# The products for h as three float32r products of split operands in place of a 20-product scheme in float32

## The chip, the core and the metric

The kernel runs on one core of one Trainium2 chip. The metric is the device time of one execution in microseconds (us). TensorE (PE) multiplies matrices out of SBUF into PSUM, which has eight banks of 128 x 512 float32; VectorE (DVE) and ScalarE (ACT) do elementwise work, GpSimd (POOL) and SyncE (SP) mostly issue DMAs. Each engine works through its own queue in order, and the queues meet only at semaphores.

## The reference

A causal convolution of seven taps over 8 sequences of 4096 tokens with 192 channels, with softmax-normalized weights for each of 8 heads of 24 channels; then a two-layer network on the 32768 tokens:

```
w = exp(weight - max); w = w / (sum(w) + 1e-9)              # 8 heads x 7 taps
y[b, s, head, :] = sum_k w[head, k] * x_pad[b, s + k, head, :]
h = y @ w_in                                                # 192 -> 2048
g = h * 1 / (1 + exp(-h))                                   # SiLU
out = g @ w_out                                             # 2048 -> 192
```

The weights w_in and w_out are handed in as 64-bit floats, x and the taps as 32-bit floats; the output is float32.

## The kernel before

The 32768 tokens are worked off in 32 stages of 1024 tokens (two halves of 512). Channels lie on partitions: x is loaded by DMA into `nat` (`load`), turned by VectorE into `xt` (`turn_in`, L617), and convolved (`conv`, L645): one product on ScalarE and six multiply-adds on VectorE for each of three slices of 64 channels, both token halves on the 128 partitions together.

*h.* The 192 input channels are three slices of 64, and the products use half the rows of the array each: two such products run beside each other on rows 0 to 63 and 64 to 127. For each of four groups g of 512 hidden columns the plain way has 24 products of 64 x 128 by 64 x 512; the kernel has 20 (`PRODUCT`, L146, issued by `product`, L725), in the manner of fast matrix multiplication. For that it forms sums of slices of x (`spread` and `win`, into `dup` and `win`), holds sums of slices of the weights (`w_own`, `w_other`, made once by `combine`), and adds and copies the products in PSUM (`micro`, L740, with the table `MICRO`), before SiLU on ScalarE writes g. Everything is native float32.

*out.* g is kept in `g_all` as 8 slots for each of two pairs of groups, of 1024 columns. Another 20-product scheme: 13 sums of slots for each pair (`SUMS`, `sum_g`, L782), 20 products for each pair (`OUT`, `out_slot`, L794), each four matrix products of 128 x 64 by 128 x 256 on column halves of the array, and 24 zeroings, copies and additions (`Dz`, `Dk`, `Dh`, `Di` ...) around them, then six turns on VectorE and eight stores. Seven of the 26 sums are not made by VectorE but by DMAs that add, issued by GpSimd (`BY_DMA`, L298).

*Order.* The instructions of a stage are written out as tokens in `PLAN` (L63): a product P, a sum s, an out product Q, a convolution tap v and so on, with a sign for the stage that it belongs to (`-` the one before, `+` the next). `step` (L862) issues them one after another, and `pin` holds each engine to that order, so the stages overlap only as the list says. The first stage is plain (`up_plain`, `down_plain`: all 24 products), since the weights are still being rounded from 64-bit words by integer operations on VectorE (`rounded`, L461) and combined; `START` (L87) is a list of its own for the passage from there into the plan. PSUM banks are handed round (`at`, L319): a bank goes back after its last use.

## Time and profile before

| | |
|---|---|
| median of three runs | 2310.18 us (2310.01 to 2311.09) |
| profiled execution, first to last instruction | 2307.9 us |
| what the median has beyond that span | 2.3 us |
| PE busy | 2288.8 us, 99% |
| VectorE busy | 2128.4 us, 92% |
| ScalarE busy | 1503.1 us, 65% |
| GpSimd busy | 234.8 us, 10% |
| granted TensorE clock | 0.997 |

All durations come from one profiled execution. A record of TensorE lasts from the first column that enters to the last result that leaves, so records overlap, and their pace is read from start to start. A float32 matrix product of the program is two records, each with its own weight load (PEld). "L730" is a line of the kernel before; the pair "64*128" names the rows and columns of the array that a product uses.

### The profile page before, as it was taken

What the parts mean: (1) busy time and instruction counts of PE and PEld (TensorE: products, weight loads), DVE (VectorE), ACT (ScalarE), POOL (GpSimd) and SP (SyncE); (2) the same over time, 40 slices, a digit from 0 to 9 for tenths busy, and PEclk for the clock granted to TensorE, in tenths of its full rate; (3) what the DMA queues carried; (4) which work ended last, traced back from release to release, by engine and by line L of the source; (5) the groups of instructions that cost most, each with busy time, mean ns of one, the idle gap of its engine ahead of it and who ended that gap; (6) DMA issues with size and microseconds to landing.
All of it is one profiled execution on the core that took longest, in us unless ns stands there. A gap on an engine that the chain in (4) does not pass through costs nothing.

```text
span 2307.9 us, 40513 instructions
## 1 busy us (share of the span) xinstructions
PE 2288.8 (99%) x15334; PEld 1377.7 (60%) x15334; DVE 2128.4 (92%) x3140; ACT 1503.1 (65%) x2957; POOL 234.8 (10%) x301
## 2 busy tenths in 40 slices
PE   9899999999999999999999999999999999999998
PEld 5255656655656656566556566566665565665664
DVE  8999999999999999999999999999999999999976
ACT  5277666676666776666776667766667766677653
POOL 4300011000011000111000110001110001100001
PEclk9999999999999999999999999999999999999999
DMA  7133355433555433555334554335553345543345
GB/s 174 26 71 74 64 104 104 85 70 68 89 104 103 76 68 66 102 104 94 68 69 81 103 103 76 72 70 93 104 98 70 69 75 103 104 80 69 71 78 92
DMA packets 465525, 195.73 MB, mean 85 GB/s; under 512 B 422000, under 2 KB 427120, under 8 KB 465328
## 3 DMA queue, kind: packets, MB, share of 16 engines
q0 software_dynamic: 31696, 115.36, 27.0%
q1 hardware_dynamic: 429440, 77.25, 19.2%
q8 instruction: 120, 1.97, 0.3%
q10 hardware_dynamic: 4192, 0.52, 0.2%
q14 instruction: 77, 0.63, 0.1%
HBM read 31.46 MB, written 25.17 MB: 25 GB/s over the span
## 4 chain that ended last, share of the span: by engine, by line
PE 95%; DVE 3%; DMA 1%; issue 0%; SPq 0%; ACT 0%; DVEq 0%; ACTq 0%; POOLq 0%
PE ps L730 48%; PE ps L800 46%; DVE u L309 2%; DVE nat L654 1%; DMA nat<-in_x_dram 1%; DMA g<-g 0%; PE ps L818 0%; DVE wd L309 0%; SPq L349 0%; DVE xt L620 0%; DMA dup<-nat 0%; DVE win L683 0%; DVE dup L683 0%; SPq L452 0%; DVE fin L775 0%
## 5 line engine op out<-in xcount | busy, mean ns | idle before, releaser
L800 PE MATMUL ps<-g,wd 128*64 128x256 f32 x9920 | 1091.3, 380 | 0.2
L800 PEld LDWEIGHTS ps<-g,wd 128*64 128x64 f32 x9920 | 703.8, 137 | 415.6 <-issue 25.8
L792 DVE TENSOR_TENSOR g<-g 128x1024 f32<-128x1024 f32 x589 | 702.0, 1218 | 24.1 <-PE ps L800 8.0
L730 PE MATMUL ps<-win,w_own 64*128 64x512 f32 x1488 | 658.4, 599 | 7.1 <-DVE win L683 6.4
L730 PE MATMUL ps<-dup,w_other 64*128 64x512 f32 x1240 | 513.0, 598 | 0.0
L730 PE MATMUL ps<-dup,w_own 64*128 64x512 f32 x1240 | 487.4, 595 | 0.0
L730 PE MATMUL ps<-win,w_other 64*128 64x512 f32 x992 | 475.1, 596 | 0.3 <-ACT g L764 0.3
L654 DVE SCALAR_TENSOR_TENSOR nat<-xt,turned,nat 128x512 f32<-128x512 f32 x558 | 399.7, 745 | 0.9 <-ACT nat L651 0.9
L766 ACT ACTIVATE ps<-ps 128x512 f32<-128x512 f32 (+1 forms) x465 | 254.3, 547 | 208.0 <-PE ps L800 175.6
L777 ACT ACTIVATE g<-ps 128x512 f32<-128x512 f32 x620 | 364.1, 603 | 18.0 <-DVE g L780 10.8
L780 DVE TENSOR_TENSOR g<-g,ps 128x512 f32<-128x512 f32 x496 | 331.1, 680 | 11.6 <-PE ps L730 8.2
L730 PEld LDWEIGHTS ps<-win,w_own 64*128 64x128 f32 x1488 | 251.4, 186 | 148.4 <-issue 61.5
L730 PEld LDWEIGHTS ps<-dup,w_own 64*128 64x128 f32 x1240 | 203.4, 186 | 140.7 <-issue 46.5
L780 DVE TENSOR_TENSOR ps<-u,ps 128x512 f32<-128x512 f32 x372 | 254.0, 691 | 33.4 <-PE ps L730 16.5
L786 POOL DMA_DIRECT2D g<-g x217 | 187.7, 913 | 945.8 <-DVE g L792 369.4
L764 ACT COPY u<-ps 128x512 f32<-128x512 f32 x341 | 200.1, 588 | 52.6 <-PE ps L730 48.7
L730 PEld LDWEIGHTS ps<-dup,w_other 64*128 64x128 f32 x1240 | 189.8, 185 | 71.4 <-ACT ps L766 42.4
L730 PEld LDWEIGHTS ps<-win,w_other 64*128 64x128 f32 x992 | 179.8, 186 | 85.3 <-issue 65.3
L777 ACT ACTIVATE g<-g 128x512 f32<-128x512 f32 x372 | 211.4, 625 | 4.5 <-DVE g L780 3.0
L766 ACT ACTIVATE fin<-ps 128x256 f32<-128x256 f32 x93 | 35.5, 382 | 214.7 <-PE ps L800 214.7
L780 DVE TENSOR_TENSOR fin<-fin,ps 128x256 f32<-128x256 f32 x248 | 94.1, 409 | 85.9 <-PE ps L800 84.7
L764 ACT COPY ps<-ps 128x512 f32<-128x512 f32 (+1 forms) x217 | 120.5, 556 | 73.8 <-PE ps L800 57.6
(92 smaller groups left out, 1166.8 us busy)
## 6 DMA issues: line engine op xcount, KB each, us to landing
g<-g POOLq DMA_DIRECT2D x217, 512.0 KB, 5.2
nat<-in_x_dram SPq DMA_DIRECT2D x382, 64.0 KB, 3.3
out_dram<-fin SPq DMA_DIRECT2D x244, 96.0 KB, 5.0
dup<-nat SPq DMA_DIRECT2D x97, 128.0 KB, 2.3
win<-nat SPq DMA_DIRECT2D x62, 128.0 KB, 2.3
fin<-in_moe_w_in_dram SPq DMA_DIRECT2D x8, 192.0 KB, 5.0
w_other<-w_own POOLq DMA_DIRECT2D x8, 192.0 KB, 7.3
g<-in_moe_w_out_dram SPq DMA_DIRECT2D x4, 384.0 KB, 7.0
```

The source lines that it names most:

```text
L309: return lambda *args, **kw: pin(getattr(self.engine, name)(*args, **kw))
L654: nc.vector.scalar_tensor_tensor(out=dst, in0=src, scalar=tap, in1=dst, op0=ALU.mult, op1=ALU.add)
L730: nc.tensor.matmul(at(b, "bank", to, g), raw(g, w, e), rows(slot_of(b, x_), e), start=first, stop=True, skip_group_check=True,)
L764: pin(nc.scalar.copy(seen[to], seen[u]))
L766: pin(nc.scalar.activation(seen[to], seen[u], AF.Copy, scale=-1.0))
L777: pin(nc.scalar.activation(seen[to], seen[u], AF.Silu, scale=float(sign)))
L780: pin(nc.vector.tensor_tensor(seen[to], seen[u], seen[v], op=op))
L786: nc.gpsimd.dma_start(out=flat(g_all[:, q, to]), in_=flat(g_all[:, q, u + v - to]), accum_op=ALU.add)
L792: pin(nc.vector.tensor_tensor(to, u, v, op=ALU.add if sign > 0 else ALU.subtract))
L800: nc.tensor.matmul(acc[R * h : R * h + R, 0:HT], wd[:, 2 * q + e, w, :], g_all[:, q, slot, e, ts(h, HT)], start=False, stop=True, skip_gro ...
```

## The change

The h products no longer use the 20-product scheme. Each value of y and of w_in is split into a high part of 12 bits and the rest, and kept three times, in the type float32r: the high part (index 0), the low part (1; for the weights times 4096) and a scaled difference (2). For each tile of h the product of the parts 0 and the product of the parts 1 are added in a PSUM bank (token A for the first 128 channels, C for the last 64), ScalarE multiplies the bank by 1 + 1/4096 in place (X), the product of the parts 2 is added (B for 128 channels, E for 64), and ScalarE applies SiLU (S). Written out, that is the whole product. A and B use the whole array; C and E use 64 rows for each token half, beside each other. A tile of h is 128 columns by 512 tokens; there are 32 in a stage (group j, chunk c, half n), so a stage has 32 tokens each of A, B, X and S, and 16 each of C and E.

The first 128 channels of x are now one tile over all 1024 tokens (`nat0`, `xt0`, `xs0`), the last 64 one with the two token halves on the partition halves (`nat1` ...). The convolution has six multiply-adds of 1024 columns and six of 512. `split` makes the three parts of y: one product on ScalarE (hx), a subtraction (lx) and a multiply-subtract (dx) on VectorE. The sums of x, the sums of weights of w_in and all additions and copies for h are gone. `round_in` splits the weights of a group after rounding them, and for the last 64 channels copies them to the other rows by DMA.

The out products, their sums, and their additions are as before, but all 26 sums of g are on VectorE. The token order of the stage is new. `START` is gone: the first stage is three-product for h and plain for out, then the whole convolution of the second stage comes, and the plan runs from stage 1 on.

```diff
     PLAN = (
+        "A.000 A.010 +i.1 -Dj9.0 A.021 A.011 A.020 A.001 C.02 +ha.2 C.01 +v.10 -s11.1 X.021 C.00  "
+        "dx.0 X.010 +ld.1 X.020 X.011 -Q4.1 +ld.0 X.001 +ld.3 -Q17.0 -Q4.0 -Q17.1 X.000 E.01  "
+        "E.02 E.00 -Di14_9.0 B.011 B.021 -DS15.0 B.020 -Di12_9.0 -Di17_f.0 A.031 S.021 B.001  "
+        "A.101 A.030 B.000 S.011 +i.0 B.010 A.100 S.001 S.020 A.120 +v.00 S.000 A.121 C.12 C.03  "
+        "S.010 +v.11 C.10 +v.01 A.110 +v.02 X.120 A.111 X.121 X.100 X.101 +v.03 X.031 X.030  "
+        "B.121 B.120 B.100 B.101 E.12 +v.12 S.120 E.10 C.11 S.100 X.111 S.121 X.110 E.03 B.031  "
+        "A.201 S.031 B.030 S.101 A.210 +v.04 B.111 A.211 E.11 C.21 S.030 X.210 A.131 A.130 A.200  "
+        "B.110 C.13 C.20 S.111 X.211 S.110 -DS16.0 E.21 B.210 A.220 -DS13.0 B.211 A.221 X.131  "
+        "C.22 -DS14.0 -DS12.0 X.200 X.201 X.130 S.210 E.13 E.20 X.220 B.131 s1.0 B.201 B.130  "
+        "S.211 A.311 X.221 S.131 B.220 A.230 S.201 B.221 A.231 C.23 E.22 +v.05 S.130 X.231 S.220  "
+        "A.301 A.310 X.230 B.231 B.200 A.300 S.221 +v.13 C.30 S.200 X.300 E.23 +v.14 C.31 S.231  "
+        "B.230 S.230 A.331 X.301 A.320 A.330 -st.0 X.311 +v.06 X.310 A.321 +v.15 C.33 C.32 E.30  "
+        "E.31 B.310 X.330 X.331 s0.0 s2.0 X.320 X.321 B.300 B.301 B.311 B.330 B.331 B.320  "
+        "-DS17.0 S.310 +v.16 Dz0.0 S.311 B.321 E.33 E.32 S.321 S.300 s1.1 Dz3.0 Dz1.0 S.331  "
+        "S.330 Q0.0 Q11.0 Q13.0 S.320 s4.0 Q13.1 s2.1 s0.1 Q0.1 Dk15.0 S.301 Q16.0 s3.0 Q16.1  "
+        "Q2.1 Q19.0 s4.1 +hx.0 s6.0 Dk11.0 Q2.0 s3.1 Q18.1 Q19.1 Q11.1 Q1.1 s6.1 s8.0 Q18.0 s7.0  "
+        "Q14.0 Q1.0 Q8.1 +hx.1 Q8.0 s8.1 *ha.0 s9.1 Q14.1 Dk8.0 Q7.1 Q9.0 Q3.0 s7.1 +lx.1 Q9.1  "
+        "Q7.0 Dh12.0 s9.0 *ld.6 Q3.1 s10.0 *ld.7 Dk5.0 s10.1 s5.0 Q12.0 Q12.1 Di12_7.0 s5.1  "
+        "Dh15.0 Q15.1 Q6.0 +dx.1 Q6.1 -st.1 s12.0 Dh13.0 s11.0 Dk13.0 s12.1 Di15_f.0 *ld.5 Q15.0  "
+        "Dh17.0 *ld.4 Q5.1 Dh16.0 +lx.0 Dh14.0 *ha.1 *ld.2 Q10.1 Q10.0 Q5.0 Di16_11.0 Du9.0  "
+        "Di14_f.0 Di13_f.0"
     )
...
-    BY_DMA = ('s0.1', 's11.1', 's4.0', 's4.1', 's5.0', 's5.1', 's8.1')
+    BY_DMA = ()
...
+    nats = [const.tile([P, n, SQ], F32, name=f"nat{i}") for i, n in enumerate((TT // SQ, TB // SQ))]
+    xts = [const.tile([P, pad + n], F32, name=f"xt{i}") for i, n in enumerate((TT, TB))]
+    xs = [const.tile([P, 3, n], F32R, name=f"xs{i}") for i, n in enumerate((TT, TB))]
+    w_a = const.tile([P, 3, NJ, 4, P], F32R, name="w_a")
+    w_b = const.tile([P, 3, NJ, 4, P], F32R, name="w_b")
...
+    def load(b, i, queue):
+        i, small = i % 4, i // 4
+        dst = nats[small][SQ * i : SQ * i + SQ]
+        if small:
+            c = P + SQ * (i % 2)
+            queue.dma_start(out=dst, in_=x_v[2 * b + i // 2][:, :, c : c + SQ])
+        else:
+            queue.dma_start(out=dst, in_=x_w[b][:, :, SQ * i : SQ * i + SQ])
...
+    def round_in(j, part, shared, scaled_by_act):
+        lo, hi = (0, CA) if part == 0 else (CA, WC)
+        words = raw(("i", j))[:, 2 * lo : 2 * hi].rearrange("p (x c t) -> p x c t", x=2, t=2)
+        w = scratch[:, 3 * WC : 3 * WC + hi - lo]
+        rounded(w.rearrange("p (x c) -> p x c", x=2), words, shared, scaled_by_act)
+        low = rest[:, 0 : hi - lo]
+        if part == 0:
+            parts = [(slice(0, P), slice(0, 4))]
+        else:
+            parts = [(slice(R * a, R * a + R), slice(2 * a, 2 * a + 2)) for a in range(2)]
+        for p_, c_ in parts:
+            to = [flat(ws[part][p_, v, j, c_, :]) for v in range(3)]
+            act.activation(to[0], w[p_], AF.Copy, scale=BELOW)
+            vec.tensor_tensor(low[p_], w[p_], f32(to[0]), op=ALU.subtract)
+            act.activation(to[1], low[p_], AF.Copy, scale=SPLIT)
+            vec.scalar_tensor_tensor(
+                out=to[2], in0=f32(to[0]), scalar=1.0 / SPLIT, in1=low[p_], op0=ALU.mult, op1=ALU.subtract
+            )
+        if part:
+            for a in range(2):
+                pool.dma_start(
+                    out=f32(rows(w_b, 1 - a)[:, :, j, 2 * a : 2 * a + 2, :]),
+                    in_=f32(rows(w_b, a)[:, :, j, 2 * a : 2 * a + 2, :]),
                 )
...
+    def split(b, k, what, src=None, cols=None):
+        cols = cols or slice(0, (TT, TB)[k])
+        src = flat(nats[k]) if src is None else src
+        hi, lo, di = (xs[k][:, v, cols] for v in range(3))
+        if what == "h":
+            act.activation(hi, src, AF.Copy, scale=BELOW)
+        elif what == "l":
+            vec.tensor_tensor(lo, src, f32(hi), op=ALU.subtract)
+        else:
+            vec.scalar_tensor_tensor(
+                out=di, in0=f32(lo), scalar=SPLIT, in1=f32(hi), op0=ALU.mult, op1=ALU.subtract
+            )
+
+    def mm(to, lhs, rhs, start=False):
+        pin(nc.tensor.matmul(to, lhs, rhs, start=start, stop=True, skip_group_check=True))
+
+    def h_bank(b, j, c, n):
+        return at(b, f"h{j}{c}{n}", 6)
+
+    def up(b, what, j, c, n=None):
+        if what == "A":
+            to = h_bank(b, j, c, n)
+            for v in range(2):
+                mm(to, w_a[:, v, j, c, :], xs[0][:, v, ts(n, TB)], start=v == 0)
+        elif what == "B":
+            mm(h_bank(b, j, c, n), w_a[:, 2, j, c, :], xs[0][:, 2, ts(n, TB)])
+        elif what in "CE":
+            to = [h_bank(b, j, c, n) for n in range(2)]
+            for v in range(2) if what == "C" else (2,):
+                for n in range(2):
+                    mm(to[n], rows(w_b, n)[:, v, j, c, :], rows(xs[1], n)[:, v, :])
+        elif what == "X":
+            to = h_bank(b, j, c, n)
+            if f"X.{j}{c}{n}" in ON_DVE:
+                vec.tensor_scalar(to, to, scalar1=1.0 + 1.0 / SPLIT, scalar2=None, op0=ALU.mult)
+            else:
+                act.activation(to, to, AF.Copy, scale=1.0 + 1.0 / SPLIT)
+        else:
+            act.activation(g_slot(j, c, n), h_bank(b, j, c, n), AF.Silu)
...
-    def product(b, r, g):
-        e, w, x_, to = PRODUCT[r]
-        first = r in FRESH and (b, g, to) not in begun
-        begun.add((b, g, to))
-        pin(
-            nc.tensor.matmul(
-                at(b, "bank", to, g),
-                raw(g, w, e),
-                rows(slot_of(b, x_), e),
-                start=first,
-                stop=True,
-                skip_group_check=True,
-            )
-        )
-
...
+    GROUPS = [(j, (c, c + 1)) for j in range(NJ) for c in (0, 2)]
+    for i in range(len(GROUPS) + 1):
+        now = GROUPS[i] if i < len(GROUPS) else (0, ())
+        was = GROUPS[i - 1] if i else (0, ())
+        if i % 2 == 0 and i // 2 + 1 < NJ:
+            for part in range(2):
+                round_in(i // 2 + 1, part, False, False)
+            load_out(0, sync) if i == 0 else None
+        for name, (j, cs) in (("A", now), ("B", was)):
+            for c in cs:
+                for n in range(2):
+                    step(0, f"{name}.{j}{c}{n}")
+        for name, (j, cs) in (("E", was), ("C", now)):
+            for c in cs:
+                step(0, f"{name}.{j}{c}")
+        for name, (j, cs) in (("S", was), ("X", now)):
+            for c in cs:
+                for n in range(2):
+                    step(0, f"{name}.{j}{c}{n}")
+    load_out(1, sync)
+    load_out(2, sync)
+    for q in range(NJ):
+        round_out(q, False, False)
+        if q == 0:
+            load_out(3, sync)
+    rest_of = sorted(prep, key=lambda t: (PREP.index(t.split(".")[0]), t))
+    first_ = [t for t in rest_of if t.split(".")[0] == "ld"]
+    first_ += ["ha.0", "i.0", "ha.1", "i.1", "ha.2"]
+    first_ += [t for t in rest_of if t.split(".")[0] == "v"]
+    first_ += ["hx.0", "lx.0", "dx.0", "hx.1", "lx.1", "dx.1"]
+    for t in first_:
+        step(1, t)
+    for t in plan:
+        if t[0] == "*":
+            step(0, t)
+    accs = [homes[k] for k in range(NK)]
...
+    for k in range(NK):
+        homes.append(homes.pop(0))
+        act.copy(plain[:, k, :], accs[k])
+    for k in range(NK):
+        vec.transpose(flat(osb_all[:, 2 * k : 2 * k + 2, :]), plain[:, k, :])
+        store_out(0, k)
+    combine_out(0, 1)
+    for b in range(1, NB + 3):
+        for t in plan:
+            step(b, t)
```

817 lines of the change are left out of this document (225 added, 592 removed), and 115 rows, old and new, of tables (COMBINE, COMBINE_OUT, MICRO, OUT).

## Prediction

> **What bounds the kernel now.** I read the page first (shares, clock, chain that ended last), then one stage in the middle by windows, then the order of TensorE's records inside it.
>
> ```profile
> span 2307.9 us, 40513 instructions
> ...
> PE 2288.8 (99%) x15334; PEld 1377.7 (60%) x15334; DVE 2128.4 (92%) x3140; ACT 1503.1 (65%) x2957; POOL 234.8 (10%) x301
> ...
> PEclk9999999999999999999999999999999999999999
> ...
> PE 95%; DVE 3%; DMA 1%; issue 0%; SPq 0%; ACT 0%; DVEq 0%; ACTq 0%; POOLq 0%
> PE ps L730 48%; PE ps L800 46%; DVE u L309 2%; DVE nat L654 1%; DMA nat<-in_x_dram 1%; DMA g<-g 0%; PE ps L818 0%; DVE wd L309 0%; SPq L349 0%; DVE xt L620 0%; DMA dup<-nat 0%; DVE win L683 0%; DVE dup L683 0%; SPq L452 0%; DVE fin L775 0%
> ```
>
> The chain is TensorE: products for h (L730) and products for out (L800), half each, at full clock. Three windows show one stage of 1024 tokens, its long run of h products, and its long run of out products (columns: stretch, its length, then busy time and count of each engine):
>
> ```profile
> 1033.12:1103.37 70.25, 70.25 (x482) 42.86 (x481) 65.62 (x96) 47.27 (x94) 6.16 (x8) 1.00 0.47 85
> 1033.12:1064.54 31.43, 31.43 (x146) 18.77 (x145) 30.42 (x50) 28.03 (x54) 0.11 (x1) 1.00 0.04 10
> 1067.47:1097.84 30.37, 30.37 (x282) 20.01 (x281) 29.52 (x36) 12.69 (x29) 5.19 (x6) 1.00 0.94 165
> ```
>
> A stage takes 70.25 us, VectorE is busy for 65.62 of it, ScalarE for 47.27. The timeline of TensorE, then of its weight loads, around two changes between the kinds of product (columns: start, length, what):
>
> ```profile
> 1027.28 0.39 PE L800 MATMUL ps<-g,wd 128*64 128x256 f32 x2
> 1027.60 0.69 PE L730 MATMUL ps<-win,w_own 64*128 64x512 f32 x1
> 1028.13 0.59 PE L730 MATMUL ps<-win,w_own 64*128 64x512 f32 x1
> 1028.56 0.59 PE L730 MATMUL ps<-win,w_own 64*128 64x512 f32 x1
> 1028.99 0.59 PE L730 MATMUL ps<-win,w_own 64*128 64x512 f32 x1
> 1029.52 3.67 PE L800 MATMUL ps<-g,wd 128*64 128x256 f32 x32
> 1033.12 0.69 PE L730 MATMUL ps<-win,w_other 64*128 64x512 f32 x1
> ```
> ```profile
> 1027.60 0.18 PEld L730 LDWEIGHTS ps<-win,w_own 64*128 64x128 f32 x1 [0.39 <-DVE win L683]
> 1027.70 0.19 PEld L730 LDWEIGHTS ps<-win,w_own 64*128 64x128 f32 x1
> ```
>
> Three prices come from these rows. A float32 product is two records; one of 512 columns starts 0.43 after the last (28.13, 28.56, 28.99), beside its twin on the other 64 rows of the array. So one column costs 0.84 ns per record. The 32 out records, 16 pairs of 256 columns, fill 1029.52 to 1033.12; in the long run 280 records take 30.37, so a pair is about 0.215. And a change of array shape costs: from out to h, 0.32 passes instead of 0.215 before the next record (27.28 to 27.60), and that record's successor comes 0.53 later instead of 0.43, because the first weights load only then (loads at 27.60 and 27.70, 0.10 to 0.11 apart). I take 0.204 (0.097 and 0.107). From h to out it is 28.99 to 29.52, 0.52 less 0.43, and a load of half as many columns, by estimate 0.053: 0.145.
>
> **The parts of the change.** *Products for h.* Out go 80 products per stage, 160 records, 80 pairs of 0.43: 34.4 us. In come, per stage, 32 A tokens with two products and 32 B with one, all on 128 rows and 512 columns, and 16 C tokens with two and 16 E with one pair of products on 64 rows: 96 full products and 48 pairs. No row shows a float32r product, so its price is bounded: above by one float32 record, 0.43, below by half of it, 0.215. I take 0.215, since each float32 product shows as two records with two weight loads, which I read as the two parts of the weights, and the same two parts of the other operand account for the doubled time inside a record; an operand that is one part already needs one of the four. That makes 96 x 0.215 + 48 x 0.215 = 31.0 us. Full-height loads of 128 columns are hidden at this pace in the warm-up (starts (0.81 - 0.38)/2 = 0.215 apart):
>
> ```profile
> 5.33 0.81 PE L578 MATMUL ps<-zeros 128*128 128x256 f32 x3
> ```
>
> The Trainium skill ("FP8 and Floating Point Precision", TensorE Precision Notes) says that true FP32 makes four passes through the array, high and low parts by each other, and that reduced precision truncates to FP22; by it one product of 512 columns would be a quarter of 0.86, the same 0.215, and no run here has shown it yet.
>
> *Changes of shape.* The old stage has six, three into each shape (1029.52 and 1033.12 above are two of them): 3 x 0.204 + 3 x 0.145 = 1.0. In the new plan TensorE's tokens fall into 23 runs: full height (A, B), two 64-row halves (C, E), two 64-column halves (Q). That is 23 changes per stage: 21 into shapes with 128 columns, 2 into Q. Nineteen are between full height and halves, which no row shows; I bound them by zero and 0.204 and take 0.204, the row of the nearest kind. Sum: 21 x 0.204 + 2 x 0.145 = 4.6 us. The Trainium skill ("TensorEngine Tiling (Array Packing)", Key Properties) says that changing the tiling mode, not just the tile, drains TensorE. It speaks against this change, and the 0.32 against 0.215 above agrees with it for the one kind of change that the trace has.
>
> *Out products* stay: 160 pairs x 0.215 = 34.4.
>
> *Stage:* 31.0 + 4.6 + 34.4 = 70.0 us, if TensorE never waits. By the same prices the old one is 34.4 + 1.0 + 34.4 = 69.8, so some 0.4 of its 70.25 is waits and small change.
>
> *VectorE and ScalarE.* Rows of their groups, and of ScalarE's real pace:
>
> ```profile
> L792 DVE TENSOR_TENSOR g<-g 128x1024 f32<-128x1024 f32 x589 | 702.0, 1218 | 24.1 <-PE ps L800 8.0
> L654 DVE SCALAR_TENSOR_TENSOR nat<-xt,turned,nat 128x512 f32<-128x512 f32 x558 | 399.7, 745 | 0.9 <-ACT nat L651 0.9
> L777 ACT ACTIVATE g<-ps 128x512 f32<-128x512 f32 x620 | 364.1, 603 | 18.0 <-DVE g L780 10.8
> L780 DVE TENSOR_TENSOR fin<-fin,ps 128x256 f32<-128x256 f32 x248 | 94.1, 409 | 85.9 <-PE ps L800 84.7
> ```
> ```profile
> 1049.75 0.58 ACT L766 ACTIVATE ps<-ps 128x512 f32<-128x512 f32 x1
> 1050.24 1.08 ACT L777 ACTIVATE g<-ps 128x512 f32<-128x512 f32 x2
> ```
>
> VectorE loses the 28 additions of h (L780), the copies and six sums of x; it gains the seven sums of g that went by DMA. Left are 26 x 1.22 = 31.7 for g, convolution 6 x 0.745 + 6 x 1.28 (twice the columns, at 1.04 ns each, an estimate) = 12.2, the splits 1.9 + 2.0, nine additions 3.7, transposes and the rest 5: 56 us, under 65.62 now and 14 under the stage. Between the last S and the next A, 19 sums, the splits and eight additions lie beside 31 Q (26.6 us): at mean durations 30.5, at the pace of back-to-back instructions some 7% less, and five more Q ahead of it give the slack. ScalarE has 32 X and 32 S, both at 512 columns. By mean durations that is 32 x (0.59 + 0.60) = 38 us; by starts, 1049.75 to 1050.24 for one kind and (1.08 - 0.60) = 0.48 for the other, it is 31. In the part of the stage where they fall TensorE has 31.0 + 4 Q (3.4) + 22 changes (4.4) = 39 us. ScalarE's 31 and 2.6 of convolution and zeroing lie under it, since instructions that do not wait start at the shorter pace. Walking the token order with these prices, each product's bank comes back before its turn, by 0.1 to 0.2 us at the tightest. So I add no wait. The seven g sums by DMA cost TensorE nothing now (POOL 10%) and taking them away gives nothing; the POOL queue keeps one small halo copy. On SP the loads of x shrink from 12 to 8 per stage, the copies of x to other rows go, and the stores stay, off the chain.
>
> **Start and end.** Rows before (rounding of weights, down products, first long run, last product):
>
> ```profile
> 12.31 4.69 DVE L654 SCALAR_TENSOR_TENSOR nat<-xt,taps,nat 128x512 f32<-128x512 f32 x6 [0.84 <-ACT nat L651]
> 16.92 0.49 DVE L309 TENSOR_SCALAR u<-g 128x256 int32<-128x256 int32 x2
> ...
> 19.60 0.50 DVE L309 TENSOR_SCALAR u<-g 128x256 int32<-128x256 int32 x2
> ...
> 22.30 1.03 DVE L309 TENSOR_SCALAR u<-g 128x768 int32<-128x768 int32 x2
> ...
> 34.34 1.03 DVE L309 TENSOR_SCALAR u<-fin 128x768 int32<-128x768 int32 x2
> ...
> 41.09 2.96 DVE L309 TENSOR_SCALAR u<-u 128x768 int32<-128x768 int32 x6
> ```
> ```profile
> 59.68 35.41 PE L818 MATMUL ps<-g,wd 128*64 128x512 f32 x164
> ...
> 120.03 0.69 PE L730 MATMUL ps<-win,w_other 64*128 64x512 f32 x1
> ```
> ```profile
> 2228.89:2307.90 79.01, 68.66 (x474) 42.09 (x472) 52.41 (x76) 39.02 (x78) 6.05 (x7) 0.96 0.38 68
> ```
> ```profile
> L800 PE MATMUL ps<-g,wd x9920: 379/379/430, 151.8 to 2297.4; 128*64 128x256 f32 x199
> ```
> ```profile
> w_other<-w_own POOLq DMA_DIRECT2D x8, 192.0 KB, 7.3
> ```
>
> Old: 120.03, then 30 stages of (2228.89 - 120.03)/30 = 70.30, then 79.0. New: VectorE rounds and splits the weights of four groups first. A group took 6.75 (34.34 to 41.09) for 768 columns, 2.7 for 256; in two parts with splits and ScalarE's answers I estimate 12.3. The order gives about 9 (data), 6.2 (first part), 5.5 (second convolution; the six took 4.69), 7.7 (second part and x splits), then 3 x 12.3: the last weights are ready at 67. The copy to the other rows lands 7.3 to 8 later, 75; the rest of h takes 7; the down products, 192 records at 35.41/164, take 41.4: stage 1 begins at 123. VectorE's further rounding ends before that, about 109. The tail stays 2307.9 - 2297.4 = 10.5.
>
> **Sum.** 123 + 31 x 69.93 (the stage unrounded) + 10.5 = 2301. The median of the runs, 2310.18, is 2.3 above the profiled span, so 2304 in the runs' measure.
>
> **The rivals.**
> *Changes between full height and 64-row halves are cheap.* For: both shapes have 128 columns, and the one change measured is between row halves and column halves. Against: nothing in the trace. If only one of the two parts is paid, 19 x 0.1 goes: 2304 - 31 x 2.0 = 2242. If none is, 19 x 0.204 = 3.9 goes and ScalarE's 33.6 in a first part of 35 lets waits of up to 1.0 return: 2304 - 31 x 2.9 = 2214. The Trainium skill ("TensorE: Matmul & The Clock Gate", Weight-path perf modes) says that weights of 128 columns load faster when the type is not FP32, with no win at four bytes; if float32r counted as such a type it would halve the 0.107 or better and lead to the same 2242; no run here shows it.
> *TensorE waits for ScalarE (slower).* Each bank of h goes to ScalarE twice, X in the middle and S at the end, with eight banks in all; a late X stops all later products. For: the margins are 0.1 to 0.2 us, and by mean durations ScalarE needs 38 + 2.6 = 40.6 against 39. Against: the pace of 0.49. It decides from 0.35 us of waits per stage on; with the 0.4 that the old stage has, 2316, with 1.6 (40.6 less 39), 2354.
> *A float32r product costs 0.43.* Then h is 62: 2304 + 31 x 31 = 3265. Against: the two weight loads per product.
>
> **How the numbers follow.** My sum has 0.42 (own range 2285 to 2325), cheap changes 0.27, waits 0.20, slow products 0.06, a start longer or shorter than worked out 0.05. Within 0.2% of 2310 (2305.6 to 2314.8) is about what a measurement cannot tell from no change. My sum lies at its edge: of its 0.42, 0.23 is faster, 0.10 the same, 0.09 slower. Cheap changes are all faster; waits are 0.02 same, 0.18 slower. Faster 0.52, same 0.12, slower 0.36. The range runs from 2210 (cheap changes) to 2350 (waits of 1.5).
>
> **What would show it.** Right: float32r records 0.215 apart, 96 x 2 per stage; starts 0.31 apart at changes and the next one late by 0.1; a stage of 70.0; stage 1 beginning near 123; VectorE at 80%, ScalarE at 65%. Wrong: records 0.43 apart, changes without a gap, or loads that wait for X (ps<-ps) for more than 0.35 us per stage.

## The result, and the profile after

The changed kernel takes 2402.42 us (median of four runs, 2402.17 to 2405.49) against 2310.10 us for the kernel before on the same chip: a ratio of 1.0403, 95% interval 1.0389 to 1.0418. It is 4.0% slower. The forecast of 2304 us had the wrong sign, and the range of 2210 to 2350 did not hold the time. The profiled execution has a span of 2400.8 us.

The page of the kernel after, the lines that answer to those of before:

```profile
span 2400.8 us, 38915 instructions
...
PE 2348.5 (98%) x16300; PEld 1548.5 (64%) x16300; DVE 1715.4 (71%) x2081; ACT 1323.8 (55%) x2678; POOL 22.4 (1%) x58
...
PEclk8899999999999999999999999999999999999999
...
PE 96%; DVE 2%; ACT 1%; DMA 0%; issue 0%; SPq 0%; DVEq 0%; ACTq 0%
...
L138 DVE TENSOR_TENSOR g<-g 128x1024 f32<-128x1024 f32 x806 | 945.7, 1218 | 411.8 <-ACT g L138 408.5
...
L138 ACT ACTIVATE g<-ps 128x512 f32<-128x512 f32 x1024 | 567.7, 606 | 125.0 <-PE ps L442 123.6
```

TensorE is still the chain, now for 96% of the span. VectorE has more room, as forecast: its sums of g wait (412 us, nearly all for values of g from ScalarE). ScalarE's SiLU in turn waits for TensorE (124 us). So the loss is in TensorE's own time or at the edges. Four windows of the same kernel show which: one stage in the middle, stage 1, everything before it, and everything from the start of the last stage (columns: stretch, length, busy time and count of PE, PEld, DVE, ACT, POOL, granted clock, DMA share, GB/s):

```profile
364.30:436.49 72.19, 72.19 (x514) 48.20 (x512) 52.49 (x61) 40.96 (x83) 0.58 (x1) 1.00 0.14 23
139.64:219.91 80.27, 71.22 (x482) 47.36 (x480) 56.60 (x75) 41.55 (x84) 0.58 (x1) 0.94 0.12 20
0.00:139.64 139.64, 107.74 (x428) 52.80 (x428) 97.10 (x182) 58.46 (x118) 8.76 (x22) 0.88 0.31 71
2313.52:2400.80 87.28, 75.94 (x546) 50.41 (x544) 42.07 (x56) 37.42 (x77) 0.00 (x0) 0.96 0.12 19
```

TensorE is busy for all of the 72.19 us of the middle stage, at full clock. So there is no wait in it, and yet it is 2.26 us longer than the forecast of 69.93. Stage 1 begins at 139.64, not at 123, and it is long. Set against the forecast of 2301.3 us for the span, the difference of 99.5 comes out so, to rounding: 31 stages times 2.26 make 70.1; the start makes 16.6; stage 1, which has no out products of a stage before it (four Q, 3.7 us), should have been 72.2 - 3.7 = 68.5 and is 80.3, 11.8 more; the end (87.3, less a stage, the four Q and the 10.5 of the forecast) makes 0.9.

The 2.26 is in the rows of TensorE's timeline (start, length, shape, records) inside a stage:

```profile
373.35 4.37 PE L442 MATMUL ps<-xs,w_a 128*128 128x512 f32 x18
377.65 1.66 PE L442 MATMUL ps<-xs,w_b 64*128 64x512 f32 x12
379.24 2.10 PE L442 MATMUL ps<-xs,w_a 128*128 128x512 f32 x8
381.27 0.97 PE L442 MATMUL ps<-xs,w_b 64*128 64x512 f32 x6
```

From start to start, 18 full-height records and a change take 4.30 us, 8 records and a change 2.03. The ten records between them cost 2.27, 0.227 each, where I had put 0.215; what is left of the short run, 2.03 - 8 x 0.227 = 0.21, is the change, where I had put 0.204. The six pairs on row halves (12 records) take 1.59: at 0.227 each, 0.23 for the change.

The start is in ScalarE's timeline (the last column is the idle time before, and who ended it):

```profile
64.32 2.07 ACT L138 ACTIVATE g<-ps 128x512 f32<-128x512 f32 x4 [1.44 <-PE ps L442]
66.25 2.10 ACT L138 ACTIVATE ps<-ps 128x512 f32<-128x512 f32 x4
68.36 0.63 ACT L138 ACTIVATE w_a<-g 128x512 fp32r<-128x512 f32 x1
69.75 0.63 ACT L138 ACTIVATE w_a<-g 128x512 fp32r<-128x512 f32 x1 [0.76 <-DVE g L138]
```

and in VectorE's waits between 28 and 138 us (us in total, times, longest):

```profile
DVE g L138 <- ACT w_a L138: 9.5, 3, 5.4
```

The scaling in `round_in` that VectorE waits for (w_a<-g at 68.36) stands on ScalarE behind four SiLU and four X of the round before, which wait for TensorE at 64.32. TensorE in turn gets its weights only from that rounding. The three engines hand one round to each other.

Stage 1 is in the timelines of ScalarE and VectorE:

```profile
151.15 0.19 ACT L138 COPY xt<-xt 64x6 f32<-64x6 f32 x1 [10.80 <-DVE xt L138]
```
```profile
141.02 9.07 DVE L138 TENSOR_TENSOR wd<-wd 128x256 f32<-128x256 f32 x23
150.00 0.49 DVE L138 TENSOR_SCALAR wd<-wd 128x256 f32<-128x256 f32 x2
150.41 1.83 DVE L138 STREAM_TRANSPOSE xt<-nat 128x512 f32<-128x512 f32 x2
```

VectorE first combines the output weights (25 instructions, `combine_out`, 9.5 us) and only then makes the transpose of the next stage (i.1). ScalarE stands for 10.8 us at the halo copy behind it (ha.2), and the rescalings X behind that copy are late: TensorE waits 8.9 us for one. Behind that wait its granted clock is 0.50 from 148 to 157.5 us; it works again from 153.11 on, so by estimate half of 4.4 us, some 2.2, are lost to the clock, and with the wait that is nearly all of the 11.8.

### The profile page after: what moved, and what is told of

The parts are those of the page before. It is cut to its first block, busy times and chain, and to the rows that moved or that the text cites. A ratio compares the mean times of both kernels' runs of the same rounds, so it can differ in the third digit from the quotient of the medians.

```text
span 2400.8 us, 38915 instructions
## 1 busy us (share of the span) xinstructions
PE 2348.5 (98%) x16300; PEld 1548.5 (64%) x16300; DVE 1715.4 (71%) x2081; ACT 1323.8 (55%) x2678; POOL 22.4 (1%) x58
## 4 chain that ended last, share of the span: by engine, by line
PE 96%; DVE 2%; ACT 1%; DMA 0%; issue 0%; SPq 0%; DVEq 0%; ACTq 0%
PE ps L442 96%; DVE g L138 1%; ACT g L138 0%; ACT ps L138 0%; ACT w_b L138 0%; DMA g<-in_moe_w_in_dram 0%; DVE nat L138 0%; SPq L138 0%; DVE fin L138 0%; DVE xs L138 0%; DMA nat<-in_x_dram 0%; DVE wd L138 0%; ACT w_a L138 0%; ACT nat L138 0%; DVE xt L138 0%
## 5 line engine op out<-in xcount | busy, mean ns | idle before, releaser
L138 DVE TENSOR_TENSOR g<-g 128x1024 f32<-128x1024 f32 x806 | 945.7, 1218 | 411.8 <-ACT g L138 408.5
L442 PE MATMUL ps<-g,wd 128*64 128x256 f32 (+1 forms) x10112 | 1127.2, 384 | 2.0 <-DVE g L138 2.0
L138 ACT ACTIVATE ps<-ps 128x512 f32<-128x512 f32 (+1 forms) x1117 | 580.9, 575 | 499.8 <-issue 273.8
L442 PE MATMUL ps<-xs,w_a 128*128 128x512 f32 x3072 | 801.1, 406 | 30.2 <-ACT g L138 12.0
L442 PEld LDWEIGHTS ps<-xs,w_a 128*128 128x128 f32 x3072 | 556.0, 189 | 258.1 <-issue 81.7
L138 ACT ACTIVATE g<-ps 128x512 f32<-128x512 f32 x1024 | 567.7, 606 | 125.0 <-PE ps L442 123.6
L442 PE MATMUL ps<-xs,w_b 64*128 64x512 f32 x3072 | 454.0, 417 | 9.1 <-ACT ps L138 9.1
L138 DVE SCALAR_TENSOR_TENSOR nat<-xt,taps,nat 128x512 f32<-128x512 f32 (+1 forms) x378 | 367.2, 1004 | 82.2 <-ACT nat L138 78.4
L442 PEld LDWEIGHTS ps<-xs,w_b 64*128 64x128 f32 x3072 | 263.2, 185 | 172.3 <-issue 113.0
L138 DVE STREAM_TRANSPOSE fin<-fin 128x256 f32<-128x256 f32 (+1 forms) x189 | 73.0, 424 | 16.8 <-ACT fin L138 16.5
L138 ACT ACTIVATE xs<-nat 128x512 fp32r<-128x512 f32 (+1 forms) x63 | 53.1, 842 | 10.9 <-DVE nat L138 10.9
```

The source lines that it names most:

```text
L138: return lambda *args, **kw: pin(getattr(self.engine, name)(*args, **kw))
L442: pin(nc.tensor.matmul(to, lhs, rhs, start=start, stop=True, skip_group_check=True))
```

## The experiments

### The pace of one record

Two kernels with trains of one kind of record over loaded data. The core of the first:

```diff
+    # 2 float32r, full height, 512 columns
+    for _ in range(48):
+        full(wr, xr)
+    # 3 float32r, full height, 256 columns
+    for _ in range(48):
+        full(wr, xr, 256)
...
+    # 5 float32r, two halves of rows
+    for _ in range(48):
+        half(wr, xr)
```

`full` issues one product on 128 rows, `half` a pair on the two 64-row halves. The other trains are written in the same way.

> Pace of the product records alone. All of the real work is left out; TensorE runs trains of records of one kind over loaded data, with the other engines idle: float32 full height 512 columns; float32r full height 512 columns; float32r full height 256 columns; bfloat16 full height 512 columns; pairs of 64-row halves in float32r, bfloat16 and float32; float32r with a change of shape after every two records; and at last float32r full height again while VectorE and ScalarE work. Theory 1 (the surplus belongs to the float32r record itself): 227 to 236 ns a record with the engines idle too, bfloat16 at 215; at 256 columns either 107 + 12 to 20 = 119 to 128 (a fixed surplus per record) or 113 to 118 (a surplus per column). Theory 2 (the surplus is contention with the other engines for the operands): 215 while they are idle, 227 to 236 only in the last train. Theory 3 (the surplus comes from the shape changes around the records): 215 in the pure trains, more only in the mixed one. In all of them a change of shape costs about 0.2 us above the plain pace: next start 0.32 us after the last, its successor 0.1 us late.

Measured, 226.5 us in all, the work of the kernel left out. Rows of TensorE's timeline, each from the middle of a train: float32r 512 columns, float32r 256 columns, bfloat16 512, then pairs on 64-row halves in float32r, bfloat16 and float32, and last float32r 512 while VectorE adds:

```profile
32.63 7.64 PE L48 MATMUL ps<-xr,wr 128*128 128x512 f32 x33
41.76 4.48 PE L48 MATMUL ps<-xr,wr 128*128 128x256 f32 x36
47.62 8.58 PE L48 MATMUL ps<-xb,wb 128*128 128x512 bf16 x39
59.66 7.64 PE L48 MATMUL ps<-xr,wr 64*128 64x512 f32 x66
69.78 8.58 PE L48 MATMUL ps<-xb,wb 64*128 64x512 bf16 x78
79.48 19.05 PE L48 MATMUL ps<-x,w 64*128 64x512 f32 x88
115.62 9.72 PE L48 MATMUL ps<-xr,wr 128*128 128x512 f32 x42
```

The granted clock is 1.00 in all of these trains. A train of n records (or pairs, which start together) lasts n - 1 paces and one record's own length (mean 0.38 to 0.41 at 512 columns, 0.28 at 256, 0.59 for float32). That gives, for float32r, (7.64 - 0.39) / 32 = 0.227 a record and 0.227 a pair; with 256 columns (4.48 - 0.28) / 35 = 0.120; for bfloat16 (8.58 - 0.38) / 38 = 0.216; for pairs of float32 records (19.05 - 0.59) / 43 = 0.429, twice 0.215; a float32 product has two of them. Under VectorE it is (9.72 - 0.39) / 41 = 0.228. So the surplus is there with all other engines idle, which rules out contention with them; it is there without a change of shape; and of the three types it belongs to float32r alone. It is 11 to 12 ns at 512 columns, and 12 at 256 if bfloat16 takes half of 0.216 there, which no train measured: a fixed amount for each record, not one for each column.

The Trainium skill ("TensorE: Matmul & The Clock Gate", section "Wait — 56ns, not 53.3ns?") gives the warm pace as columns by 2.4 GHz and some 2.5 ns, 215.7 for 512 columns. The bfloat16 trains agree with it (0.216) and the float32r trains do not (0.227); for this type the measurement decides.

The second kernel of this kind, also with the work left out, looked at other sizes, at the length of runs between changes, and at a handover that the last experiments need:

```diff
+    for run in (1, 4, 8, 16):
+        for _ in range(max(2, 16 // run)):
+            for _ in range(run):
+                full(wr, xr)
+            for _ in range(run):
+                half(wr, xr)
...
+        one = wr[64:65, c, 0:1]
+        pin(nc.gpsimd.tensor_copy(one, one))
+        for n in (0, 1):
+            mm(banks[n], rows(wr, 1 - n)[:, c, :], rows(xr, 1 - n)[:, 512 * n : 512 * n + 512])
```

> Pace of float32r records again, with all of the real work left out: full height at 384 and 128 columns; 64 columns of weights; 32 records added up in one bank; float32 out products; changes of shape after every 1, 4, 8 and 16 records; and one bank written by the two halves of rows in turn, ordered by a one-number copy on GpSimd. Theory 1 (a fixed surplus of 12 to 13 ns per float32r record, found at 256 and at 512 columns): 384 columns 172 to 174 ns, 128 columns 64 to 68, 64 columns of weights again 226, one bank again 226. Theory 2 (the surplus hangs on the weights that are loaded): with 64 columns of weights the pace falls to 215 to 221. For the runs: Theory 1 says that the first ten or so records after a change are irregular at 231 on average and that a change costs 0.2 us whatever the length of the run; rival: the cost of a change falls for longer runs, since the queue of weight loads has refilled. The ordered crossing should take 0.5 to 1.0 us from the last record on one half to the first on the other.

Rows of its timeline: 384 columns, then 64 columns of weights:

```profile
30.68 4.15 PE L70 MATMUL ps<-xr,wr 128*128 128x384 f32 x23
...
44.73 5.65 PE L70 MATMUL ps<-xr,wr 128*64 128x512 f32 x24
```

With 384 columns a record takes (4.15 - 0.33) / 22 = 0.174, where 384 columns at the bfloat16 rate would take 0.162: again 12 ns. Half the weights do not help: (5.65 - 0.39) / 23 = 0.229. Nor does one bank for all records (0.227). So the surplus does not hang on the weights loaded. With 128 columns the expectation failed: the starts are 0.111 apart, not 0.064 to 0.068; something else bounds so short a record, and what it is stays open. Weight loads (one for each record or pair) around the changes, runs of 1, 4, 8 and 16, each run's first and that of the next run:

```profile
62.90 0.19 PEld L48 LDWEIGHTS ps<-xr,wr 128*128 128x128 f32 x1 [0.25 <-issue]
63.33 0.18 PEld L48 LDWEIGHTS ps<-xr,wr 64*128 64x128 f32 x2 [0.24 <-issue]
...
75.29 0.77 PEld L48 LDWEIGHTS ps<-xr,wr 64*128 64x128 f32 x8 [0.37 <-issue]
76.42 0.76 PEld L48 LDWEIGHTS ps<-xr,wr 128*128 128x128 f32 x4 [0.36 <-issue]
...
85.24 1.70 PEld L48 LDWEIGHTS ps<-xr,wr 64*128 64x128 f32 x16 [0.36 <-issue]
87.31 1.70 PEld L48 LDWEIGHTS ps<-xr,wr 128*128 128x128 f32 x8 [0.36 <-issue]
...
95.34 3.52 PEld L48 LDWEIGHTS ps<-xr,wr 64*128 64x128 f32 x32 [0.35 <-issue]
99.21 3.52 PEld L48 LDWEIGHTS ps<-xr,wr 128*128 128x128 f32 x16 [0.35 <-issue]
```

Runs of 1, 4, 8 and 16 with their change take 0.43, 1.13, 2.07 and 3.87. From 1 to 4 and from 4 to 8 a record adds 0.233 and 0.235, from 8 to 16 only 0.225. So a change costs 0.20 at once, whatever the run, and its first eight or so records run at 0.233 to 0.235. The plan has 144 slots for h (a slot is a full-height record or a pair) and 23 changes a stage, six slots to a run. At 0.227 to 0.234 a slot and 0.20 a change its h part is 37.3 to 38.3 us; the stage has 72.19 less 34.5 for the out products (160 pairs at 0.216; the longest run of them, from 405.26 on, has 144 pairs in 31.30 us), 37.7. So of the 2.26 us the surplus that every float32r record has (0.227 less 0.215, 144 times) makes 1.7, and the slower records behind changes some 0.4.

### The start

```diff
-            act.activation(to[0], w[p_], AF.Copy, scale=BELOW)
+            vec.tensor_scalar(to[0], w[p_], scalar1=BELOW, scalar2=None, op0=ALU.mult)
...
-            act.activation(to[1], low[p_], AF.Copy, scale=SPLIT)
+            pool.tensor_scalar(to[1], low[p_], scalar1=SPLIT, scalar2=None, op0=ALU.mult)
```

> Only the rounding of the input weights in stage 0 is changed: its two scalings move from ScalarE to VectorE (the high part) and GpSimd (the scaled low part), so that they don't queue behind the rescaling (X) and SiLU (S) steps there. Theory (the late start of stage 1, at 139.6 us instead of 123, comes from that queue on ScalarE): VectorE's waits of 3.4 and 5.4 us in the rounding go, the last group is rounded near 72, stage 1 begins 8 to 14 us earlier (126 to 132), the time is 8 to 14 us under that of the changed kernel (2388 to 2394), and the steady stage of 72.2 us doesn't move. Rival (TensorE has too much work there, whatever the queue): stage 1 still begins within 3 us of 139.6, and the time is 2399 to 2405.

Measured 2391.50 us (2390.82 to 2392.37), ratio to the kernel before 1.0354 (1.0337 to 1.0371): 10.9 under the changed kernel. The first A of stage 1, in the timeline of this run:

```profile
129.47 1.89 PE L442 MATMUL ps<-xs,w_a 128*128 128x512 f32 x7
```

It is 10.2 earlier. VectorE's waits for w_a and w_b are gone from its list, and the stage is 72.19 as before. The queue on ScalarE was the cause for 10 of the 16.6 us. TensorE still waits 8.2 us in stage 0 for the copies of the weights to the other rows, in three places; the forecast had those in it (the last copy lands at 75, and TensorE goes on at 74.36). Where the other six are, this run's timeline shows: from there the rest of h takes 12.2 us instead of 7, with a wait of 1.5 in it and a granted clock of 0.54 up to 80 us, and the down products take 43.0 instead of 41.4, at a clock of 0.53 for their first 3.5 us. The forecast had full clock for both.

### Stage 1

```diff
-    combine_out(0, 1)
     for b in range(1, NB + 3):
         for t in plan:
             step(b, t)
+            if b == 1 and t == "+ha.2":
+                combine_out(0, 1)
```

> Only the 25 combinations of the output weights on VectorE (9.4 us) are moved: from before the first step of stage 1 to behind the step ha.2 in it, so that the transpose i.1 and the halo copy ha.2 of the next stage don't wait for them. Theory (ScalarE stands at ha.2 for 10.8 us behind VectorE's combinations, and TensorE behind ScalarE's rescaling X): TensorE's stall of 8.9 us near 153 goes, stage 1 lasts 69 to 73 us instead of 80.3, the time is 8 to 11 us under that of the changed kernel (2391 to 2394). Rival (the stage is long because of something else, and the combinations only move the wait to the sums and the out products): stage 1 stays at 78 or more and the time within 3 us of 2402.

Measured 2394.14 us (2393.26 to 2396.32), ratio 1.0368 (1.0352 to 1.0383): 8.3 less. Stage 1 in windows of this run:

```profile
139.53:211.93 72.40, 70.07 (x482) 46.03 (x480) 56.59 (x75) 41.52 (x84) 0.58 (x1) 1.00 0.13 22
```

The stage is 7.9 shorter, at full clock (0.94 before). The theory holds for that much; 72.4 is still 3.9 above what a stage without a predecessor needs, of which 2.3 are waits for X and S.

Both together:

> The changed kernel with both repairs at the start: the scalings of the rounding moved from ScalarE to VectorE and GpSimd, and the 25 combinations of the output weights moved behind the step ha.2 of stage 1. Theory (two separate delays before the steady part): the 10.9 and 8.3 us add, 2381 to 2386; the stage stays 72.19. Rival (an earlier start only lets stage 1 wait longer): 2388 to 2392. By neither does it come to the kernel before, since the 1.9 us a stage are left.

Measured 2383.55 us (2383.08 to 2384.91), ratio 1.0321 (1.0305 to 1.0336). The gains add (18.9 of 10.9 + 8.3), and the kernel is still 3.2% slower than before. Most of what is left is the stage: 31 x (72.19 - 70.30) = 58.6 of the 74 us.

### The stage without the changes of shape

The products on 128 rows as pairs on row halves, with new tokens for the second half, and a new order of the stage:

```diff
-                mm(to, w_a[:, v, j, c, :], xs[0][:, v, ts(n, TB)], start=v == 0)
...
+                        w, x_ = rows(w_a, e)[:, v, j, c, :], rows(xs[0], e)[:, v, ts(n, TB)]
+                    mm(to, w, x_, start=what == "A" and v == 0)
```

Here e is the bank's own half n, for the new tokens G and H as for A and B: this kernel leaves out the products with the other rows, and has as many records as the whole product needs.

> The products on 128 rows (A, B) are issued as pairs on 64-row halves of the array like C and E, so that the 19 changes between full height and halves leave the stage, with a new order of the same steps (4 changes a stage instead of 23). To keep each PSUM bank with one half of the rows, the second pair of A and of B reads the same rows of weights and x again instead of the other rows: that part of the contraction is wrong, and everything else is issued as in the changed kernel; the number of record slots on TensorE (144 a stage for h) is the same. Theory 1 (a stage is record pace plus shape changes): 144 x 0.227 to 0.232 + 34.4 + 4 x 0.2 = 67.9 to 68.6 us a stage instead of 72.2, the time 110 to 135 us under that of the changed kernel: 2267 to 2292. Theory 2 (the changes are covered by other waits, or ScalarE or VectorE bounds as soon as TensorE is faster): a stage stays between 70.5 and 72.2, the time at 2350 to 2402.

Measured 2344.83 us (2344.41 to 2347.10), ratio 1.0154 (1.0137 to 1.0171), 57.6 under the changed kernel, half of what theory 1 asks for. A stage in windows, and TensorE's waits in it:

```profile
296.25:366.39 70.14, 68.53 (x610) 50.58 (x609) 52.55 (x63) 40.37 (x83) 0.58 (x1) 1.00 0.14 24
```
```profile
PE ps L441 <- ACT fin L137: 1.6, 1, 1.6
```

TensorE's own time is 68.53, as theory 1 says: 3.66 less than 72.19, and 19 changes at 0.20 are 3.8. But one wait of 1.6 has come up in the out products, so theory 2 holds in part: the 70.14 and the 2344.83 lie between the two forecasts. The wait is taken up below.

### Halves with the right rows

To compute the real product, each bank must get products from both halves of the rows, one after the other. The order C, A on the bank's own half; G on the other half; X; H on the other half; B, E on the own half; S. Between the halves stands a copy (O, N) of one weight onto itself: it waits until the first half has read that weight, and the next half waits for the copy.

```diff
+        elif what in "ON":
+            v, p = (1, R) if what == "O" else (2, 0)
+            one = w_a[p : p + 1, v, j, c, 0:1]
+            pool.tensor_copy(one, one)
```

The handover by itself, in the second pace run (timeline of two engines):

```profile
107.56 0.51 PE L48 MATMUL ps<-xr,wr 64*128 64x512 f32 x2 [0.30 <-POOL wr L108]
108.14 0.17 POOL L112 CAST wr<-wr 1x1 fp32r<-1x1 f32 x1 [0.63 <-PE ps L48]
...
108.36 0.49 PE L48 MATMUL ps<-xr,wr 64*128 64x512 f32 x2 [0.30 <-POOL wr L112]
```

It takes 0.80 (107.56 to 108.36) from pair to pair here and some 0.87 in the next six, less than four pairs of other banks (later ones take 1.16, at a granted clock of 0.50).

> The 64-row halves with the right rows: per bank first C and A on the bank's own half, then G (the other rows of A) on the other half, X, then H (the other rows of B), B and E. Between the halves a copy of one weight onto itself on GpSimd (O, N) puts them in order, 0.87 us from pair to pair in the pace run; the order of the steps is new, and 12 of the 32 rescalings X go to VectorE. Theory (record pace and shape changes make the stage): 144 x 0.229 + 34.4 + 4 changes = 68.5 to 69.0 us a stage if the orderings are covered by other products, time 2270 to 2315 with the same start as the changed kernel (139 to 146) and a long stage 1. Rival (the orderings cost what they save, since products of other banks do not cover them): 16 x 2 orderings at 0.1 to 0.3 us, 70.5 to 75 us a stage, time 2340 to 2490.

> The halves in order, and both changes at the start: scalings of the rounding on VectorE and GpSimd, and the 25 combinations of the output weights in nine parts spread over the first half of stage 1. If the gains add, the stage is that of the halves in order, stage 1 begins near 130 and is no more than 3 us longer than the later ones: 130 + 31 x 68.7 to 69.2 + 3 + 12 = 2275 to 2290, under both kernels. Rival (the three work on the same waits and do not add): no more than 8 us under the halves in order alone.

Measured: 2412.50 us (2411.10 to 2414.65), ratio 1.0444 (1.0426 to 1.0461), and with both repairs 2411.33 (2410.27 to 2413.57), ratio 1.0442 (1.0426 to 1.0458). The rivals had the times: a stage takes 71.94, and the gains did not add, since TensorE had new waits for the copies in stages 0 and 1 (27.4 and 25.7 us up to 230 us). The waits of the weight loads in one stage of the first of the two, the group of the copies, and one of them beside VectorE:

```profile
PEld ps L444 <- POOL w_a L140: 4.6, 8, 1.0
```
```profile
L140 POOL CAST w_a<-w_a 1x1 fp32r<-1x1 f32 x1024 | 361.7, 360 | 1880.5 <-PE ps L444 1866.5
```
```profile
345.29 0.55 POOL L140 CAST w_a<-w_a 1x1 fp32r<-1x1 f32 x1 [1.82 <-PE ps L444]
...
344.58 1.22 DVE L140 TENSOR_TENSOR g<-g 128x1024 f32<-128x1024 f32 x1
```

The copy of one number takes 0.18 in most rows and 0.36 on average. The one at 345.29 lasts 0.55 and ends at 345.84, 0.04 after VectorE's sum of two operands in SBUF (344.58 + 1.22 = 345.80). All nine copies above 0.4 us in this stage end so, 0.04 to 0.05 after a convolution step, a split or a sum; beside VectorE's X, its transposes and its additions from PSUM they take 0.18. The Trainium skill ("SBUF — State Buffer", section "SBUF: two separate sides") states it: VectorE with two inputs from SBUF and GpSimd share a port pair, and whoever comes first keeps it for the whole instruction. The trace agrees.

> The halves in order once more. The run before it lost 3 us a stage because a one-number copy on GpSimd takes 0.2 us beside most instructions of VectorE but lasts to the end of one that reads two operands from SBUF (convolution, sums of g, splits), up to 1.2 us. Here the order of the steps is made with that in view, 24 of the copies are spread over VectorE, ScalarE and GpSimd by what runs there, one is left out since the waits for X and S order the halves anyway, 14 of the rescalings X go to VectorE, and stage 0 keeps the forms of the changed kernel; both repairs of the start are in. Theory (GpSimd's copies behind VectorE were the whole loss): 68.3 to 69.3 us a stage, stage 1 from 130, 2262 to 2300 in all, under the kernel before. Rival (the ordering costs the same on any engine, since its round trip of 0.8 us is not covered): 70.5 to 72 a stage, 2330 to 2380.

Measured 2341.69 us (2341.30 to 2344.16), ratio 1.0138 (1.0121 to 1.0155). A stage takes 70.17, 1.8 less than in the run with all copies on GpSimd, but not the 68.3 to 69.3 of the theory; the time is in the rival's range. The copies on GpSimd that were left still waited in the same way, 2.6 us a stage at the weight loads, and X on VectorE held up stages 0 and 1 (22 us):

```profile
PEld ps L448 <- POOL w_a L144: 2.6, 5, 0.7
```

> The same once more without a copy on GpSimd in the plan: the order between the halves comes from copies on ScalarE (12) and VectorE (15) and, at 5 places, from the waits that are there anyway; 13 rescalings X go to VectorE, from stage 2 on only; the 25 combinations of the output weights are in 13 parts. In the run before, three of GpSimd's copies a stage still lasted 1.2 us behind a convolution step, and stages 0 and 1 waited 22 us for rescalings on VectorE. Theory (that was the loss): 68.4 to 69.2 us a stage, stage 1 from 126 to 131 and no longer than the rest, 2255 to 2285 in all, under both kernels. Rival (VectorE and ScalarE are too full in the h part for the copies): 69.8 to 71 a stage, 2305 to 2340.

Measured 2345.51 us (2345.09 to 2346.43), ratio 1.0154 (1.0140 to 1.0168): over both ranges, with a stage of 70.79 as the rival has it. Stage 1 begins at 128.25, the waits for GpSimd are gone, and the wait of 1.6 us of the halves run is back. TensorE's waits in the whole run, and VectorE, ScalarE and TensorE around one:

```profile
PE ps L450 <- ACT fin L146: 50.0, 31, 1.6
```
```profile
420.89 1.41 DVE L146 TENSOR_TENSOR fin<-fin,ps 128x256 f32<-128x256 f32 x4 [0.47 <-PE ps L450]
...
421.67 0.66 ACT L146 ACTIVATE fin<-ps 128x256 f32<-128x256 f32 x2 [3.43 <-DVE fin L146]
...
422.38 1.95 PE L450 MATMUL ps<-g,wd 128*64 128x256 f32 x16 [1.61 <-ACT fin L146]
```

ScalarE's two copies out of banks (Dh17, Du9) start when the second of VectorE's four additions (Di16) is done, and TensorE's next Q when the second copy is. Dh17 takes nothing from Di16: both only read one bank, ob6, and Di16 stands first in the plan. The list of waits says "fin", but no value passes between the two.

> The same with two mends. The stage of the run before waited 1.6 us on TensorE for a copy out of a bank on ScalarE (Dh17) that stood behind an addition on VectorE (Di16) which only reads the same bank; the new order keeps no such pair one behind the other. Stage 1 (83.8 us) waited for the loads and transposes of stage 2, which stood behind the stores of stage 0 in SP's queue; they are issued before the down products now. Theory (two readers of one PSUM bank are put in order, and this was the wait): 68.3 to 69.1 us a stage, stage 1 within 3 us of the others, from 126 to 131, 2255 to 2280 in all, under both kernels. Rival (the wait at the end of the stage belongs to VectorE's sums, whose order is much the same): 70 to 71 us a stage, 2320 to 2340.

The ends of the two orders, and the steps put before the down products:

```diff
-        "Dh16.0 s5.1 +lx.1 +lx.0 Q6.1 Q6.0 Q10.0 *ld.5 Q10.1 *ld.2 Dk13.0 Q5.1 *ld.7 Dh14.0 s0.1 "
-        "Q5.0 +dx.1 s5.0 s11.0 *ha.1 Di13_f.0 Di16_11.0 Di14_f.0 *ld.4 Dh17.0 Di15_f.0 *ld.6 "
-        "Du9.0"
+        "Q10.1 s5.1 Dh15.0 Q15.0 Q6.0 Q15.1 s0.1 Dh16.0 s5.0 Q6.1 -st.0 Dk13.0 Dh14.0 Di16_11.0 "
+        "Q10.0 s11.0 Q5.0 Di14_f.0 +dx.1 *ld.4 Du9.0 *ld.5 Q5.1 Di15_f.0 Dh17.0 *ld.6 *ld.2 "
+        "*ld.7 Di13_f.0 -st.1"
...
+    for t in [t for t in rest_of if t.split(".")[0] == "ld"] + ["ha.0", "ha.1", "i.1", "i.0", "ha.2"]:
+        step(2, t)
```

Measured 2279.45 us (2277.46 to 2279.64), ratio to the kernel before 0.9865, interval 0.9849 to 0.9882: 1.35% faster than before and 5.1% faster than the changed kernel. A stage, and stage 1, in windows:

```profile
341.90:410.58 68.68, 68.68 (x611) 50.06 (x610) 62.41 (x94) 37.41 (x82) 0.19 (x1) 1.00 0.15 24
127.95:204.45 76.50, 72.42 (x594) 51.16 (x593) 59.02 (x97) 42.86 (x93) 1.49 (x1) 0.98 0.13 22
```

No wait of TensorE is left in the stage. Stage 1 has lost 7.3 of its 83.8 us but is not within 3 us of the rest. The expectation told the order wrongly in one point: Di16 still stands before Dh17 in it, and what may help is that Du9, for whose bank TensorE waits, now stands before Dh17. So many other steps moved that the reason was not yet separated. The last run goes back to the kernel with the wait and exchanges that one pair:

```diff
-        "Q5.0 +dx.1 s5.0 s11.0 *ha.1 Di13_f.0 Di16_11.0 Di14_f.0 *ld.4 Dh17.0 Di15_f.0 *ld.6 "
+        "Q5.0 +dx.1 s5.0 s11.0 *ha.1 Di13_f.0 Dh17.0 Di16_11.0 Di14_f.0 *ld.4 Di15_f.0 *ld.6 "
```

> The kernel with the 1.6 us wait at the end of each stage (the third in which the halves are put in order), with one exchange in the plan and nothing else: Dh17 (a copy out of bank ob6 on ScalarE) now stands before Di16 (an addition on VectorE that reads ob6 too). In the faster kernel after it that pair kept its order; there Du9, for whose bank TensorE waits, came to stand before Dh17 on ScalarE. Theory (two readers of one PSUM bank follow each other in the order of the plan, so ScalarE waited for VectorE): the wait goes, 69.1 to 69.3 us a stage instead of 70.8, 2292 to 2302 in all instead of 2345.5. Rival (Dh17 waited for something else, VectorE's sums or the bank's products): 70.5 to 70.9 a stage, 2340 to 2347.

Measured 2289.57 us (2288.68 to 2290.16), ratio 0.9911 (0.9895 to 0.9928), 56 us under the kernel with the pair the other way round, a little more than expected. One stage:

```profile
278.05:346.85 68.80, 68.80 (x610) 51.53 (x608) 63.08 (x90) 36.77 (x82) 0.19 (x1) 1.00 0.15 24
```

The theory holds: 1.8 to 1.9 us a stage for one exchange of a copy and an addition that share nothing but the bank that they read. The instruction records of the two traces also tell who sets the order. In the kernel with the wait, Dh17's record has a wait for the semaphore that VectorE raises as its instructions end: it is raised at 421.65, behind Di16, and Dh17 starts at 421.67. After the exchange Dh17's record has no wait at all, and Di16's has one for ScalarE's semaphore. So the program orders the two readers; what the chip would do without these semaphores no run here shows.

## Why the prediction was wrong

*What bounds the kernel* was right: TensorE before and after.

*Products for h: failed, and it is the largest term.* "I take 0.215" was the lower end of the bounds that I had given. The pace is 0.227 in long trains and up to 0.234 in the first eight records after a change, which is where this plan has most of its records. With the rest of the stage near the forecast that is most of the 2.26 us a stage and of the 70 of 99 us. With 0.227 to 0.234 in its place, the same working gives 71.7 to 72.7 a stage, and a kernel slower than before. It took the time out of the range; the sign would have been wrong without it too, since start and stage 1 add 28 us and the forecast lay only 6 under the kernel before. The reading behind the step, that a float32r product takes a quarter of a float32 one, came near (0.227 of 0.86); that it has no cost of its own beside that was an assumption from rows of another type (the warm-up at 0.215 was float32, with 256 columns).

*Changes of shape: right.* 0.20 to 0.23 each in the rows of the stage and 0.20 in the pace run, against 0.204, and 19 fewer of them saved 3.66 us a stage; the rival of cheap changes (0.27) was wrong. What the price did not contain are the slower records behind a change, some 0.4 us a stage.

*Out products: right*, 34.5 against 34.4.

*VectorE and ScalarE: right in the steady stage.* No wait on TensorE is left in it, with VectorE at 52.5 and ScalarE at 41.0 of 72.2 us (73% and 57%; I had said 80 and 65). The rival of waits for ScalarE (0.20) is wrong there, though stage 1 has such a wait. The time does lie above its 2316 to 2354, but for other reasons. That the sums moved from DMAs to VectorE cost nothing fits the absent waits; no run tried it alone.

*Start: failed.* I counted ScalarE's answers as a delay, not as instructions in a queue behind SiLU and X of the round before. That made 10 of the 16.6 us. Without that queue (first repair) stage 1 begins at 129.5; the rest is the end of h in stage 0 and the head of the down products, both at a lower granted clock than I had taken. The terms that I listed up to the last weights also add up to 65.3, not to the 67 that I went on with. I gave a different start 0.05.

*Stage 1: a step was missing.* I noted that VectorE's further rounding ends before the start, and took all 31 stages for equal. The 25 combinations of the output weights come after the down products, at the head of VectorE's queue for stage 1, and behind them stand i.1, then ha.2 and the rescalings X on ScalarE. Stage 1 was 11.8 us too long; moving the combinations gave back 8.3 in the time.

*End: right*, to 0.9 us.

## What to carry to other kernels

Price a record by a train of its own type and size before the sum hangs on it: a surplus of 12 ns in 215 was the largest part of the miss, since there are 144 such slots in each of 31 stages. Changes of array shape cost 0.2 us each here, so a tiling that keeps to one shape can be worth more than the whole surplus (here 3.7 us a stage for 19 changes, about their price). At the edges of a pipeline look for one-off work at the head of an in-order queue, and for short answers of one engine queued behind long work of another. Where two engines read one bank, look whether the program makes one wait for the other, and put first the one on which more depends.

## What the runs showed of the hardware that I had not expected

- float32r records have a fixed surplus of about 12 ns over bfloat16 records and over half a float32 record (0.120, 0.174 and 0.227 at 256, 384 and 512 columns), with idle engines and with busy ones, with 128 and 64 columns of weights. What makes it is open.
- After a change of shape about eight float32r records run at 0.233 to 0.235 in the pace run before the pace settles at 0.225 to 0.227.
- float32r records of 128 columns came 0.111 apart.
- A one-number copy on GpSimd takes 0.18 us, or up to 1.27 to the end of VectorE's instruction, when that reads two operands from SBUF.
- After TensorE's wait of 8.9 us in stage 1 of the changed kernel its granted clock was 0.50 until 157.5 us, 4.4 us after it went on; in the run without that wait the clock of stage 1 was 1.00.
